# Scores from 64 rows per head in two PSUM banks, and token groups of 384 instead of 256

## The chip, the cores and the metric

The kernel runs on one core of one Trainium2 chip. The metric is the device time of one execution in microseconds. The core has TensorE (PE in the profile, with its weight loads as PEld), VectorE (DVE), ScalarE (ACT), GpSimd (POOL) and SyncE (SP), which here only issues DMA transfers. Matmuls write to PSUM, which has eight banks of 512 fp32 values in each of 128 partitions.

## The reference

Four batches, eight heads, 768 tokens, head size 64. Each token attends to the keys closer than 16 positions and to 24 block summaries (the maximum over 32 keys, the mean over 32 values); then comes a two-layer unit over all 3072 tokens.

```python
k_sum = k.reshape(B, H, nb, block, D).max(axis=3)       # block 32, nb 24
v_sum = v.reshape(B, H, nb, block, D).mean(axis=3)
scores_l = scale * np.matmul(q, k.transpose(0, 1, 3, 2))
mask_l = np.abs(pos[:, None] - pos[None, :]) < window   # window 16
scores_s = scale * np.einsum('bhsd,bhnd->bhsn', q, k_sum) + np.log(block)
a = softmax(concat(where(mask_l, scores_l, -1e9), scores_s))
attn = np.matmul(a, concat(v, v_sum))
x = attn.transpose(0, 2, 1, 3).reshape(B * S, H * D)    # 3072 x 512
out = np.maximum(x @ w1, x @ w2) @ w_out                # d_ff 1024
```

## The kernel before

**Tiles.** The work goes by batch, by pair of heads (four pairs), and within a pair by groups of 256 tokens (three of them). `prep` casts k and q to bf16 (`kqb`, line 340), turns them by TensorE (line 359) so that the 64 features of one head lie in partitions 0 to 63 and those of the other in 64 to 127, and places k in `kx` (line 373) and q in `qx` (line 388). `kx` holds for each tile of 64 keys 96 columns: 64 keys, 24 block maxima, 8 zeros; a window of 128 columns thus covers 64 keys, the summaries, and 32 keys of the next tile.

`qx` has two planes per head pair: in plane 0 the rows of the second head are zero, in plane 1 those of the first. The zeros are set once (lines 216 and 217). So one matmul of 128 rows gives the scores of both heads: the weights are the 128 columns of `kx`, and 2 x 64 queries stream through it (line 414). The last tile's queries wrap around the end of the sequence, so it takes two matmuls.

**A group.** `scores` fills one PSUM bank with 4 tiles x 2 heads x 64 queries, ACT takes the exponential of it into `pb` (line 426). Keys out of the window are hidden in one of two ways: in batch 0 by two matmuls of an identity with a pattern `hide` that is added to the scores in PSUM (line 403), in the other batches by a DVE multiplication of `pb` with a 0/1 `mask` (lines 435 and 441). `values` multiplies by `vx` (values, block means and a column of ones; line 460), DVE takes the reciprocal of the sums (line 472) and scales (line 474), TensorE turns x (line 484) and DVE copies it to `xt` (line 489).

**Maxout.** Since max(h1, h2) = h1 + relu(h2 - h1), the kernel makes `wd` = w2 - w1 once, and `w1o` = w1 @ w_out once (lines 506 to 544). For a group of 256 tokens, `maxout` computes x @ wd in four banks of two d_ff slices of 128 each (line 560), relu by ACT into `g` (line 565), and then for each 128 tokens x @ w1o (line 574) plus g @ w_out (line 581), one copy by ACT (line 340) and one store (line 592).

**Order.** Nothing is ordered by hand. `Plan` takes every operation with an engine, an estimated duration, its buffers and a priority, plays the execution through with those durations, and then issues the operations in the order in which they started there; each engine then runs its own list strictly in order. Attention of batch b has priority 1000 b, its maxout 1000 b + 1500 (lower goes first), so maxout of one batch fills TensorE's gaps in the attention of later ones. Buffers come from a `Ring` of slots; a buffer is taken when its first writer is planned and is free after its last user. The PSUM ring has eight single banks with caps by kind: two for turning k and q, two for scores, two for values, three for maxout.

Of the kernel before, what the change touches and what calls it, by code (L numbers as in the profile page):

```python
# [19 lines left out]
class Ring:  # L20
# [3 lines left out]
    def __init__(self, slots, cap=None, turn=None):  # L24
        self.slots, self.cap, self.turn = slots, cap or {}, turn
        self.owner = [None] * len(slots)

    def find(self, buf, now):
        live = [o is not None and o.end() > now for o in self.owner]
        if buf.kind in self.cap and self.cap[buf.kind] <= sum(  # L30
                o.kind == buf.kind for o, l in zip(self.owner, live) if l):
            return None
        if self.turn is not None and buf is not self.turn[0]:
            return None
        return min((s for s, l in enumerate(live) if not l), default=None, key=lambda s: (
            -1.0 if self.owner[s] is None else self.owner[s].end()))


class Buf:


    def __init__(self, ring, kind=None):
        self.ring, self.kind, self.slot = ring, kind, None
        self.writers, self.users = [], []
# [4 lines left out]
    def take(self, slot):  # L49
        self.slot, self.ring.owner[slot] = slot, self  # L50
        if self.ring.turn is not None:
            self.ring.turn.pop(0)
# [76 lines left out]
def kernel(  # L129
# [22 lines left out]
    NP, NT, NG, GT = H // 2, S // 64, 3, 256  # L152
# [12 lines left out]
    banks = Ring(list(range(8)), {"kq": 2, "sc": 2, "av": 2, "mm": 3})  # L165
# [9 lines left out]
    qxr = Ring(tiles("qx", 4, [128, 2, S], BF16))  # L175
    pbr = Ring(tiles("pb", 12, [128, 4, 192], BF16))
# [4 lines left out]
    xsr = Ring(tiles("xs", 4, [128, 2, 2, 2, D], BF16))  # L181
    xtr = Ring(tiles("xt", 6, [128, KC, GT], BF16))
    gr = Ring(tiles("g", 3, [128, FC, GT], BF16))
# [12 lines left out]
    hide = const.tile([128, 4, 64], BF16, name="hide")  # L196
    mask = const.tile([128, 4, 64], BF16, name="mask")
# [11 lines left out]
    def fixed_parts():  # L209
# [5 lines left out]
        def zero_qx(t):  # L215
            nc.vector.memset(t[0:64, 1], 0.0)
            nc.vector.memset(t[64:128, 0], 0.0)

# [6 lines left out]
        for i, t in enumerate(qxr.slots):  # L225
            once(qxr, i, 0.9, lambda t=t: zero_qx(t), i - 1)
        for i, t in enumerate(pbr.slots):
            once(pbr, i, 0.2, lambda t=t: nc.vector.memset(t[:, :, 64:128], 0.0), i / 3 - 1)
# [5 lines left out]
        def make_hide():  # L234

            nc.gpsimd.memset(hide[:], 0.0)
            for lo, hi, base in ((0, 64, -16), (96, 128, 96 - 48)):
                keep(hide[lo:hi], base + window - 1, 1, [[0, 4], [-1, 64]])  # L240
                keep(hide[lo:hi], window - 1 - base, -1, [[0, 4], [1, 64]])
            keep(hide[64:96], nb - 1, -1, [[0, 4], [0, 64]])
            nc.gpsimd.memset(hide[0:64, 3, 48:64], NEG)
            nc.gpsimd.memset(hide[96:128, 3, 0:48], NEG)
# [99 lines left out]
    def prep(b, hp, prio, k_on, q_on):  # L344
# [41 lines left out]
        for a in range(2):  # L386
            r = slice(64 * a, 64 * a + 64)
            op("ACT", 0.8, lambda a=a, r=r: nc.scalar.copy(  # L388
                out=qx[b, hp].ap[r, a, :], in_=order(qps)[r]),
               read=[qps], write=[qx[b, hp]], prio=prio, label=f"place q{tag}")  # L390

    def scores(b, hp, grp, prio, mask_on):


        ps, pb, tag = Buf(banks, "sc"), Buf(pbr), f"{b}{hp}{grp}"

        def view():
            return bank(ps).rearrange("p (i a w q) -> p i a w q", i=2, a=2, w=2)

        def mm():  # L400
            if mask_on == "PE":
                for i in range(2):
                    nc.tensor.matmul(
                        out=view()[:, i], lhsT=identity[:],
                        rhs=(hide[:, 2 * i:2 * i + 2] if grp == NG - 1 else hide[:, 0:2]).rearrange(
                            "p (o w) q -> p o w q", o=1).to_broadcast([128, 2, 2, 64]),
                        start=(i == 0), stop=False)
            for i in range(4):
                t = 4 * grp + i
                w = kx[b, hp].ap[:, 96 * t:96 * t + 128]  # L410
                at, o = 64 * t + 16, view()[:, i // 2, :, i % 2]
                for n0, n1 in ((0, 64),) if t < NT - 1 else ((0, 48), (48, 64)):
                    c = (at + n0) % S
                    nc.tensor.matmul(out=o[:, :, n0:n1], lhsT=w,  # L414
                                     rhs=qx[b, hp].ap[:, :, c:c + n1 - n0],
                                     start=(mask_on != "PE"),
                                     stop=(mask_on != "PE" or (i == 3 and n1 == 64)))

        op("PE", 0.25 + (0.23 if mask_on == "PE" else 0), mm, read=[kx[b, hp], qx[b, hp], hide_in],
           write=[ps], prio=prio, label=f"scores {tag}")  # L420

        def pv():
            a = pb.ap[:, :, 0:128]
            return bass.AP(a.tensor, a.offset, [a.ap[0], a.ap[1], [128, 2], [1, 64]])

        op("ACT", 0.7, lambda: nc.scalar.activation(  # L426
            out=pv(), in_=bank(ps).rearrange("p (i w q) -> p i w q", w=2, q=64),
            func=ACT.Exp, bias=bias[:], scale=scale),
           read=[ps], write=[pb], prio=prio, label=f"exp {tag}")

        def hidden_out():
            eng = nc.vector if mask_on == "DVE" else nc.gpsimd
            if grp < NG - 1:
                m = mask[:, 0:1].rearrange("p w (o q) -> p w o q", o=1).to_broadcast([128, 4, 2, 64])
                eng.tensor_tensor(out=pv(), in0=pv(), in1=m, op=ALU.mult)  # L435
            else:
                o = pv().rearrange("p (i a) w q -> p i a w q", a=2)
                for i in range(2):
                    m = mask[:, 2 * i:2 * i + 2].rearrange("p (o w) q -> p o w q", o=1).to_broadcast(
                        [128, 2, 2, 64])  # L440
                    eng.tensor_tensor(out=o[:, i], in0=o[:, i], in1=m, op=ALU.mult)

        if mask_on != "PE":
            op(mask_on, 0.43 if grp < NG - 1 else 0.56, hidden_out, read=[mask_in], change=[pb], prio=prio,
               label=f"mask {tag}")
        return pb
# [3 lines left out]
    def values(b, hp, grp, pb, prio):  # L450
        ps, tag = Buf(banks, "av"), f"{b}{hp}{grp}"

        def av():
            return bank(ps)[:, 0:4 * (D + 1)].rearrange("p (u a d) -> p u a d", u=2, a=2)

        def mm():
            for u in range(2):
                for a in range(2):
                    for par in range(2):
                        nc.tensor.matmul(out=av()[:, u, a, :],  # L460
                                         lhsT=pb.ap[:, 2 * u + a, 64 * par:64 * par + 128],
                                         rhs=vx[b].ap[:, 4 * grp + 2 * u + par, 2 * hp + a, 0:D + 1],
                                         start=(par == 0), stop=(par == 1))

        op("PE", 0.24, mm, read=[pb, vx[b]], write=[ps], prio=prio, label=f"values {tag}")
# [3 lines left out]
        if hp == 0:  # L469
# [4 lines left out]
        op("DVE", 0.42, lambda: nc.vector.tensor_tensor(  # L474
            out=x.ap[:, hp % 2], in0=av()[:, :, :, 0:D],
            in1=inv.ap[:].to_broadcast([128, 2, 2, D]), op=ALU.mult),
# [5 lines left out]
        def turn():  # L482
            for n in range(4):
                nc.tensor.transpose(out=bank(xp, 512, BF16)[:, 128 * n:128 * n + 128],  # L484
                                    in_=x.ap[:, n // 2, n % 2].rearrange("p a d -> p (a d)"),
                                    identity=identity[:])

        op("PE", 0.23, turn, read=[x], write=[xp], prio=prio, label=f"turn x{tag}")
        op("DVE", 0.42, lambda: nc.vector.tensor_copy(  # L489
            out=x_t.ap[:, hp - 1:hp + 1, :].rearrange("p h n -> p (h n)"),  # L490
            in_=bank(xp, 512, BF16)), read=[xp], write=[x_t], prio=prio, label=f"xt {tag}")

    invr = Ring(tiles("inv", 3, [128, 2, 2, 1], F32))
# [58 lines left out]
    def maxout(b, grp, prio):  # L552
        x, g = xt[b, grp], Buf(gr)
        for n in range(4):
            ps = Buf(banks, "mm")

            def hid(n=n, ps=ps):
                for s in range(2):
                    for c in range(KC):
                        nc.tensor.matmul(out=bank(ps)[:, 256 * s:256 * s + 256],  # L560
                                         lhsT=wd[n].ap[:, c, 128 * s:128 * s + 128],
                                         rhs=x.ap[:, c, :], start=(c == 0), stop=(c == KC - 1))

            op("PE", 0.88, hid, read=[x, wd[n]], write=[ps], prio=prio, label=f"hidden {b}{grp}{n}")
            op("ACT", 0.6, lambda n=n, ps=ps: nc.scalar.activation(  # L565
                out=g.ap[:, 2 * n:2 * n + 2, :].rearrange("p f n -> p (f n)"), in_=bank(ps),
                func=ACT.Relu), read=[ps], write=[g], prio=-1, label=f"relu {b}{grp}{n}")
        for u in range(2):
# [43 lines left out]
    def first_attention():  # L612

        pbs = {}
        for hp in range(NP):
            prep(0, hp, hp, *FIRST[hp])
            for grp in range(NG):
                pbs[hp, grp] = scores(0, hp, grp, (10, 110, 210)[grp] + hp, "PE")
        for grp in range(NG):
            for hp in range(NP):  # L620
                values(0, hp, grp, pbs[hp, grp], (20, 120, 220)[grp] + hp)
# [54 lines left out]
```

## Time and profile before

| | |
|---|---|
| runs | 193.31 us median of 3 (192.92 to 194.15) |
| profiled execution, span from the first to the last instruction | 192.5 us |
| what lies around the span, taken as median less span | 0.8 us |
| PE busy | 166.4 us, 1643 matmuls |
| ACT, DVE busy | 114.1 us, 109.9 us |
| data read and written | 25.17 MB, 6.29 MB |
| granted TensorE clock, mean | 0.991 |

The profile page lists one execution. It has no time of that execution beside its span, so the span is set against the median of the timed runs. The 40 slices show shares of the span in tenths; the chain of waits is followed back from the last instruction to whatever released each step. Matmuls are pipelined: the duration of one in the group list is much longer than the distance between two, which is seen in the chain as the length of a run divided by its matmuls.

### The profile page before, as it was taken

How to read it: one execution, taken by the hardware profiler on the slowest of the kernel's cores; microseconds unless marked ns; L12 is line 12 of the kernel's file. 1: busy time of each engine (PE TensorE's matmuls, PEld its weight loads, DVE VectorE, ACT ScalarE, POOL GpSimd, SP SyncE). 2: the span in 40 equal slices, each digit the busy share in tenths (PEclk: the TensorE clock that was granted, in tenths of full speed). 3: DMA queues.
4: the chain of work that ended last, by engine and by line, in shares of the span. 5: the costliest groups of instructions: out<-in, count | busy, mean ns of one | idle time of the engine just before them, and what ended most of it. 6: DMA issues, size and time to landing. Idle time of an engine off the chain costs nothing.

```text
span 192.5 us, 4148 instructions
## 1 busy us (share of the span) xinstructions
PE 166.4 (86%) x1643; PEld 117.9 (61%) x1664; DVE 109.9 (57%) x289; ACT 114.1 (59%) x173; POOL 25.7 (13%) x39
## 2 busy tenths in 40 slices
PE   0629619899999969999979999999999999999990
PEld 0426419865757738758657767487696676665740
DVE  6908956888979438759868953079777600000000
ACT  2533964384689949219967955179986443342621
POOL 7556221300330003300003300000000000000000
PEclk9999996999999999999999999999999999999999
DMA  5999999999999999999999996061020111120303
GB/s 187 226 305 356 234 240 347 371 381 281 210 359 251 292 268 217 339 309 217 229 288 223 340 218 193 3 164 24 3 109 5 54 58 59 50 109 0 112 0 109
DMA packets 47859, 37.27 MB, mean 194 GB/s; under 512 B 26208, under 2 KB 43744, under 8 KB 47840
## 3 DMA queue, kind: packets, MB, share of 16 engines
q1 hardware_dynamic: 47840, 37.01, 71.8%
q8 instruction: 13, 0.21, 0.5%
q14 instruction: 6, 0.05, 0.1%
HBM read 25.17 MB, written 6.29 MB: 163 GB/s over the span
## 4 chain that ended last, share of the span: by engine, by line
PE 53%; DMA 33%; SPq 5%; DVE 4%; POOL 2%; issue 1%; ACT 0%; ACTq 0%
PE banks L581 17%; PE banks L560 16%; DMA vf<-in_v_dram 13%; DMA vx<-vb 10%; PE banks L574 7%; PE banks L460 5%; DMA wf<-in_moe_w_out_dram 4%; SPq L503 4%; DMA vx<-vx 4%; PE banks L414 3%; DMA kqf<-in_k_dram 2%; PE banks L359 2%; POOL vb L340 2%; PE banks L484 2%; PE banks L313 1%; DVE pb L435 1%
## 5 line engine op out<-in xcount | busy, mean ns | idle before, releaser
L560 PE MATMUL banks<-xt,wd 128*128 128x256 bf16 x384 | 46.6, 273 | 0.5 <-DVE xt L489 0.5
L581 PE MATMUL banks<-wo,g 128*128 128x512 bf16 x184 | 44.9, 379 | 0.4
L560 PEld LDWEIGHTS <-wd 128*128 128x128 bf16 x384 | 36.4, 98 | 6.1 <-issue 0.7
L426 ACT ACTIVATE pb<-banks,bias 128x512 bf16<-128x512 f32 x48 | 31.5, 686 | 10.2 <-PE banks L414 9.9
L565 ACT ACTIVATE g<-banks 128x512 bf16<-128x512 f32 x48 | 28.3, 596 | 13.7 <-PE banks L560 13.2
L340 ACT COPY o<-banks 128x512 f32<-128x512 f32 x24 | 14.0, 585 | 28.7 <-PE banks L581 28.4
L388 ACT COPY qx<-banks 64x768 bf16<-64x768 bf16 x32 | 25.3, 791 | 6.1 <-PE banks L359 5.8
L581 PEld LDWEIGHTS <-g 128*128 128x128 bf16 x192 | 17.2, 97 | 16.5
L460 PE MATMUL banks<-vx,pb 128*128 128x65 bf16 x384 | 19.4, 196 | 3.6 <-DMA vx<-vx 1.8
L574 PE MATMUL banks<-w1o,xt 128*128 128x512 bf16 x85 | 21.9, 379 | 0.6
L460 PEld LDWEIGHTS <-pb 128*128 128x128 bf16 x384 | 16.9, 100 | 7.1 <-DMA vx<-vx 2.1
L359 PE MATMUL banks<-identity,kqb 128*128 128x128 bf16 x192 | 16.6, 234 | 5.3 <-DVE kqb L340 4.7
L340 ACT CAST kqb<-kqf 128x768 bf16<-128x768 f32 x16 | 13.1, 830 | 13.6 <-DMA kqf<-in_q_dram 8.7
L414 PE MATMUL banks<-qx,kx 128*128 128x128 bf16 (+2 forms) x208 | 18.6, 226 | 2.3 <-ACT qx L388 1.3
L340 POOL CAST vb<-vf 128x1536 bf16<-128x1536 f32 x8 | 12.2, 1520 | 55.0 <-DMA vf<-in_v_dram 35.2
L474 DVE TENSOR_TENSOR xs<-banks,inv 128x256 bf16<-128x256 f32 x48 | 19.1, 415 | 0.3
L414 PEld LDWEIGHTS <-kx 128*128 128x128 bf16 x208 | 15.1, 103 | 6.6 <-DVE kx L382 2.4
L359 PEld LDWEIGHTS <-kqb 128*128 128x128 bf16 x192 | 13.6, 106 | 8.5 <-DVE kqb L340 4.7
L373 DVE COPY kx<-banks 128x768 bf16<-128x768 bf16 x16 | 15.2, 955 | 2.9 <-PE banks L359 1.7
L375 DVE TENSOR_REDUCE ks<-kx 128x24 bf16<-128x768 bf16 x16 | 15.1, 944 | 0.1
L489 DVE COPY xt<-banks 128x512 bf16<-128x512 bf16 x24 | 9.8, 418 | 7.2 <-PE banks L484 6.8
L574 PEld LDWEIGHTS <-xt 128*128 128x128 bf16 x96 | 8.9, 98 | 7.9
(47 smaller groups left out, 129.8 us busy)
## 6 DMA issues: line engine op xcount, KB each, us to landing
kqf<-in_k_dram SPq DMA_DIRECT2D x16, 384.0 KB, 6.6
kqf<-in_q_dram SPq DMA_DIRECT2D x16, 384.0 KB, 5.7
vf<-in_v_dram SPq DMA_DIRECT2D x8, 768.0 KB, 10.7
out_dram<-o SPq DMA_DIRECT2D x20, 256.0 KB, 2.2
wf<-in_moe_w_dram SPq DMA_DIRECT2D x8, 512.0 KB, 11.1
vx<-vb SPq DMA_DIRECT2D x6, 396.0 KB, 8.0
wf<-in_moe_w_out_dram SPq DMA_DIRECT2D x4, 512.0 KB, 8.6
vx<-vx SPq DMA_DIRECT2D x4, 363.0 KB, 6.2
```

The source lines that it names most:

```text
L340: {"DVE": nc.vector.tensor_copy, "ACT": nc.scalar.copy, "POOL": nc.gpsimd.tensor_copy}[engine](out=o, in_=i)
L359: nc.tensor.transpose(out=bank(ps, S, BF16)[:, 128 * j:128 * j + 128], in_=src.ap[:, j].rearrange("p h d -> p (h d)"), identity=identity[:])
L373: op("DVE", 0.96, lambda: nc.vector.tensor_copy(out=kt()[:, :, 0:64], in_=order(kps)), read=[kps], write=[kx[b, hp], kmain], prio=prio, la ...
L388: op("ACT", 0.8, lambda a=a, r=r: nc.scalar.copy(out=qx[b, hp].ap[r, a, :], in_=order(qps)[r]), read=[qps], write=[qx[b, hp]], prio=prio, ...
L414: nc.tensor.matmul(out=o[:, :, n0:n1], lhsT=w, rhs=qx[b, hp].ap[:, :, c:c + n1 - n0], start=(mask_on != "PE"), stop=(mask_on != "PE" or (i ...
L426: op("ACT", 0.7, lambda: nc.scalar.activation(out=pv(), in_=bank(ps).rearrange("p (i w q) -> p i w q", w=2, q=64), func=ACT.Exp, bias=bias ...
L460: nc.tensor.matmul(out=av()[:, u, a, :], lhsT=pb.ap[:, 2 * u + a, 64 * par:64 * par + 128], rhs=vx[b].ap[:, 4 * grp + 2 * u + par, 2 * hp ...
L474: op("DVE", 0.42, lambda: nc.vector.tensor_tensor(out=x.ap[:, hp % 2], in0=av()[:, :, :, 0:D], in1=inv.ap[:].to_broadcast([128, 2, 2, D]), ...
L560: nc.tensor.matmul(out=bank(ps)[:, 256 * s:256 * s + 256], lhsT=wd[n].ap[:, c, 128 * s:128 * s + 128], rhs=x.ap[:, c, :], start=(c == 0), ...
L565: op("ACT", 0.6, lambda n=n, ps=ps: nc.scalar.activation(out=g.ap[:, 2 * n:2 * n + 2, :].rearrange("p f n -> p (f n)"), in_=bank(ps), func ...
L574: nc.tensor.matmul(out=bank(ps), lhsT=x.ap[:, c, sl], rhs=w1o[c].ap[:], start=(c == 0), stop=False)
L581: nc.tensor.matmul(out=bank(ps), lhsT=g.ap[:, f, sl], rhs=wo[f // 2].ap[:, f % 2, :], start=False, stop=(f == FC - 1))
```

## The change

Three things are changed together.

- `qx` has one plane and no zeros. Scores are computed for each head by its own matmul of 64 rows (partitions 0 to 63 for one head, 64 to 127 for the other) and 64 query columns, into a PSUM bank of its own. A scores buffer is therefore two adjacent banks, and `Ring` learns to hand out such pairs.
- Attention and maxout go in two groups of 384 tokens instead of three of 256. So exp takes 768 elements per row at once, values fill 6 x 65 columns, `hide` and `mask` are 6 tiles wide; maxout takes one d_ff slice of 384 tokens per bank (eight matmul groups and eight relus instead of four), and three output tiles of 128 tokens per group instead of two.
- The numbers of buffers follow: `pb` 8 instead of 12, `xt` 4 instead of 6, `g` 2 instead of 3, each half as large again. The plan's estimated durations are set to the new sizes.

```diff
-    NP, NT, NG, GT = H // 2, S // 64, 3, 256
+    NP, NT, NG, GU = H // 2, S // 64, 2, 3
+    GT = 128 * GU
...
+        if buf.wide:
+            return min((s for s in range(0, len(live), 2) if not live[s] and not live[s + 1]),
+                       default=None, key=lambda s: max(self.freed(s), self.freed(s + 1)))
         return min((s for s, l in enumerate(live) if not l), default=None, key=lambda s: (
-            -1.0 if self.owner[s] is None else self.owner[s].end()))
+            self.pairs and not live[s ^ 1], self.freed(s)))
...
-    qxr = Ring(tiles("qx", 4, [128, 2, S], BF16))
-    pbr = Ring(tiles("pb", 12, [128, 4, 192], BF16))
+    qxr = Ring(tiles("qx", 4, [128, S], BF16))
+    pbr = Ring(tiles("pb", 8, [128, 2 * GU, 192], BF16))
...
-        def zero_qx(t):
-            nc.vector.memset(t[0:64, 1], 0.0)
-            nc.vector.memset(t[64:128, 0], 0.0)
...
-        for a in range(2):
-            r = slice(64 * a, 64 * a + 64)
-            op("ACT", 0.8, lambda a=a, r=r: nc.scalar.copy(
-                out=qx[b, hp].ap[r, a, :], in_=order(qps)[r]),
-               read=[qps], write=[qx[b, hp]], prio=prio, label=f"place q{tag}")
+        op("ACT", 0.8, lambda: nc.scalar.copy(
+            out=qx[b, hp].ap[:].rearrange("p (c j) -> p c j", j=J), in_=order(qps)),
+           read=[qps], write=[qx[b, hp]], prio=prio, label=f"place q{tag}")
...
-        ps, pb, tag = Buf(banks, "sc"), Buf(pbr), f"{b}{hp}{grp}"
+        ps, pb, tag = Buf(banks, "sc", wide=True), Buf(pbr), f"{b}{hp}{grp}"
...
-            for i in range(4):
-                t = 4 * grp + i
-                w = kx[b, hp].ap[:, 96 * t:96 * t + 128]
...
-                    nc.tensor.matmul(out=o[:, :, n0:n1], lhsT=w,
-                                     rhs=qx[b, hp].ap[:, :, c:c + n1 - n0],
...
+            for i in range(2 * GU):
+                t = 2 * GU * grp + i
                 for n0, n1 in ((0, 64),) if t < NT - 1 else ((0, 48), (48, 64)):
...
+                    for a in range(2):
+                        r = slice(64 * a, 64 * a + 64)
+                        nc.tensor.matmul(out=view()[:, a, 64 * i + n0:64 * i + n1],
+                                         lhsT=kx[b, hp].ap[r, 96 * t:96 * t + 128],
+                                         rhs=qx[b, hp].ap[r, c:c + n1 - n0],
...
-        for n in range(4):
+        for n in range(FC):
             ps = Buf(banks, "mm")
 
             def hid(n=n, ps=ps):
-                for s in range(2):
-                    for c in range(KC):
-                        nc.tensor.matmul(out=bank(ps)[:, 256 * s:256 * s + 256],
-                                         lhsT=wd[n].ap[:, c, 128 * s:128 * s + 128],
-                                         rhs=x.ap[:, c, :], start=(c == 0), stop=(c == KC - 1))
+                for c in range(KC):
+                    nc.tensor.matmul(out=bank(ps, GT), lhsT=wd[n // 2].ap[:, c, 128 * (n % 2):128 * (n % 2) + 128],
+                                     rhs=x.ap[:, c, :], start=(c == 0), stop=(c == KC - 1))
```

129 lines of the change are left out of this document (64 added, 65 removed).

## The prediction

> **What bounds the kernel now.** I read the page first: its span, the busy shares and the 40 slices; then the time windows, then TensorE's waits, then the chain of waits in order of time.
>
> ```profile
> span 192.5 us, 4148 instructions
> PE 166.4 (86%) x1643; PEld 117.9 (61%) x1664; DVE 109.9 (57%) x289; ACT 114.1 (59%) x173; POOL 25.7 (13%) x39
> ...
> PEclk9999996999999999999999999999999999999999
> DMA  5999999999999999999999996061020111120303
> ```
>
> TensorE is the busiest engine, and the transfer engines are full for the first 24 slices (115 us). A busy share over the whole span doesn't say which of the two sets the end, so I cut the span where values of batch 0 are running (34.3), where values of batch 2 begin (97.36) and where the last matmuls end (188.1).
>
> ```profile
> 0.00:34.30 34.30, 18.53 (x183) 14.40 (x184) 22.93 (x59) 17.81 (x24) 15.16 (x29) 0.95 1.03 272
> 34.30:97.36 63.06, 58.33 (x617) 41.40 (x627) 48.13 (x118) 42.77 (x64) 7.41 (x8) 1.00 1.08 288
> 97.36:188.10 90.74, 89.56 (x844) 62.13 (x855) 38.86 (x113) 52.92 (x86) 3.17 (x2) 1.00 0.38 102
> 188.10:192.50 4.40, 0.00 (x0) 0.00 (x0) 0.00 (x0) 0.58 (x1) 0.00 (x0) 1.00 0.36 119
> ```
>
> Columns are start:end, length, busy time of PE, PEld, DVE, ACT and POOL, granted clock, DMA share, GB/s. Up to 34.3 TensorE is busy for half the time and the transfers set the pace. From 34.3 on it is busy for 58.33 + 89.56 = 147.9 of 153.8 us at full clock. What it waited for there, all told:
>
> ```profile
> PE banks L460 <- DMA vx<-vx: 1.8, 1, 1.8
> PE banks L460 <- DMA kqf<-in_k_dram: 1.3, 1, 1.3
> PE banks L560 <- DVE xt L489: 0.5, 1, 0.5
> PE banks L460 <- DVE pb L435: 0.5, 1, 0.5
> PE banks L544 <- ACT wo L340: 0.4, 1, 0.4
> PE banks L313 <- POOL vb L340: 0.3, 1, 0.3
> ```
>
> 3.1 us for transfers (one at 69, one at 96 us) and only 1.7 us for DVE, ACT and POOL. So after 34.3 the amount of TensorE work sets the end nearly one for one; making DVE or ACT faster can return at most that 1.7 us. Behind the last matmul there are 4.4 us of one copy and one store, of the same size after the change.
>
> **TensorE's prices.** These are lengths of runs in the chain, thus start to start, not the pipelined durations of the page.
>
> ```profile
> 75.28 0.24 PE banks L460 x8
> 110.82 0.45 PE banks L414 x8
> 112.13 0.23 PE banks L414 x5
> 161.99 3.49 PE banks L560 x32
> 167.21 3.45 PE banks L581 x16
> 188.09 0.58 ACT o L340
> ```
>
> Per matmul with its own weight load: 65 columns (L460) 0.24/8 = 0.030 us; 128 columns (L414) 0.45/8 = 0.056; 256 columns (L560) 3.49/32 = 0.109; 512 columns (L581) 3.45/16 = 0.216. So 0.00042 us per column, (0.216 - 0.109)/256, and 0.002 besides. How far down does that go? The smallest matmul of the trace has 32 columns:
>
> ```profile
> 149.15 0.18 PE L414 MATMUL banks<-qx,kx 128*128 128x32 bf16 x1
> 149.18 0.59 PE L581 MATMUL banks<-wo,g 128*128 128x512 bf16 x2
> ```
>
> Its successor starts 0.03 us later, as behind 65 columns, though 32 columns alone would be 0.015. One load and one matmul don't go below about 0.03 us, however few the columns.
>
> **The change, part by part.**
>
> *Scores.* A head pair now takes 13 matmuls (12 tiles, the last one split), 0.45 + 0.23 = 0.68 us. Afterwards each becomes two, of 64 rows and half the columns: 26. One after another at the 0.03 of the nearest rows this is 0.78 us, +0.10. If the two of a pair, at different row positions, run beside each other, it is 13 x 0.03 = 0.39 us, -0.29. The trace has no matmul with fewer than 128 rows, so it doesn't decide; and the switch between 64 and 128 rows may have a price of its own (a rival below). I take one after another: every row of this kernel that has a load per matmul sits at 0.03 or above. How many head pairs count:
>
> ```profile
> 34.30:97.36 63.06, 5.17 (x65) 4.36 (x65) 1.00 1.08 288
> 97.36:188.10 90.74, 7.31 (x91) 5.82 (x91) 1.00 0.38 102
> ```
>
> These are the same windows for the scores line alone: 65/13 = 5 head pairs up to 97.36 and 7 behind it. So +0.10 x 12 = +1.2 us. The first 5 come ahead of values that wait for transfers anyway (1.8 and 1.3 us), so their 0.5 us is covered; without that cover it counts in full. Batch 0's four head pairs lie before 34.3 under the transfers. Its hidden-key matmuls are 16 of 384 columns in place of 24 of 256, the same 6144 columns.
>
> *Maxout.* 384 matmuls of 256 columns become 256 of 384: 0.002 + 384 x 0.00042 = 0.163 us each, 41.7 against 384 x 0.109 = 41.9: about -0.2 us. The second matmuls (L574, L581), values, transposes, weights' work and stores keep number and size.
>
> *ACT, DVE, POOL.*
>
> ```profile
> L426 ACT ACTIVATE pb<-banks,bias 128x512 bf16<-128x512 f32 x48 | 31.5, 686 | 10.2 <-PE banks L414 9.9
> L565 ACT ACTIVATE g<-banks 128x512 bf16<-128x512 f32 x48 | 28.3, 596 | 13.7 <-PE banks L560 13.2
> L388 ACT COPY qx<-banks 64x768 bf16<-64x768 bf16 x32 | 25.3, 791 | 6.1 <-PE banks L359 5.8
> L474 DVE TENSOR_TENSOR xs<-banks,inv 128x256 bf16<-128x256 f32 x48 | 19.1, 415 | 0.3
> L216 DVE MEMSET qx<- 64x384 uint32 x4 | 1.5, 378 | 0.1
> L217 DVE MEMSET qx<- 64x384 uint32 x4 | 1.5, 378 | 0.5
> ```
>
> Placing q: 16 copies instead of 32, of the same 768 elements a row, so 16 x 0.79 = 12.7 us less. Exp: 32 of 768 elements, each between 0.69 and 1.5 x 0.69 = 1.03 us, so 22 to 33 us against 48 x 0.686 = 32.9. Relu: 64 of 384, each between 0.45 and 0.60 us, 29 to 38 against 28.6. ACT gives up some 13 us, at least 3. DVE loses the zeroes of q (3.0 us, all before 9 us) and 16 of 48 normalisations that become half again as long. None of it is on the path after 34.3: in the last dense window DVE is busy for 38.9 and ACT for 52.9 of 90.7 us. I cost it at nothing; the cover is the maxout matmuls that the plan puts between. Were it gone, a longer exp or normalisation would hold a group back by up to 0.34 or 0.2 us, 14 groups behind 97.36: up to 5 us.
>
> ```profile
> 1.71 2.30 POOL L231 TENSOR_SCALAR_AFFINE_SELECT hide<-hide 64x256 bf16<-64x256 bf16 x5
> 9.25 1.47 POOL L340 CAST vb<-vf 128x1536 bf16<-128x1536 f32 x1 [1.84 <-DMA vf<-in_v_dram]
> ```
>
> The hidden-key pattern is half as wide again: up to 1.2 us more on POOL, ahead of the v cast, where POOL idles 1.84 us for v. Nothing. No DMA is added or removed.
>
> *PSUM.* A scores group takes two adjacent banks, so two groups in flight take four of eight. A group that waits for a free pair holds TensorE's whole list, the values and maxout matmuls written behind it, and ACT's exp after those. I cost it at nothing, between no effect and the rival below.
>
> *Sum.* +1.2 - 0.5 - 0.2 = about +0.5 us on a span of 192.5, so 193.0. The median of the runs, 193.31, lies 0.8 us above the span; with the same 0.8 the time is **193.8 us**: no change that can be measured (I take 1%, 1.9 us, as the limit).
>
> **Rivals.**
>
> *The pairs overlap.* 0.39 us per head pair: -0.29 x 7 = -2.0 behind 97.36, up to -1.5 before it (or that is lost in longer waits for transfers), -0.2 for maxout: 193.3 - 2.2 to 193.3 - 3.7, so 189.6 to 191.1, say **190.4**. For it: the two use different rows, operands and banks. Against: the floor of 0.03 us under the 32-column matmul looks like the load's or the issue's, and there are twice as many of both. [...]
>
> *Each switch of row height empties TensorE.*
>
> ```profile
> L460 PE MATMUL banks<-vx,pb 128*128 128x65 bf16 x384 | 19.4, 196 | 3.6 <-DMA vx<-vx 1.8
> L414 PEld LDWEIGHTS <-kx 128*128 128x128 bf16 x208 | 15.1, 103 | 6.6 <-DVE kx L382 2.4
> ```
>
> A 65-column matmul lasts 0.196 us though the next starts after 0.030, so 0.17 us of each is hidden by its successor; a switch could expose that, and the load's 0.10. After 34.3 there are 24 scores groups: 48 switches if each stands alone, 24 if two of a head pair stand together. At 0.17 that is 4 to 8 us, at 0.27 up to 13; on top of +0.5, less what the transfer waits swallow, some +4.5: **197.8**, slower. It decides from about 0.06 us a switch (36 x 0.06 = 2.2) if pairs don't overlap. Against: transposes and matmuls alternate without a visible price, but both have 128 rows. [...] With both, overlap and emptying, the sum is -3.7 + 4 to 8, so 193.6 to 197.6, say **195**.
>
> *Order.* Larger groups and bank pairs make the written-out order stall in more places. The longest wait now is 1.8 us; two more like it give **197**. Against: the waits for DVE, ACT and POOL are 1.7 us in all.
>
> **How the numbers follow.** One after another without a price of switching, 0.35; overlap alone, 0.30; emptying alone, 0.15; both, 0.12; order, 0.08. Faster by over 1% (below 191.4): nine tenths of the overlap case and a little of the forecast, 0.30. Slower (above 195.2): emptying, half of both, most of the order case and a little of the forecast, 0.30. Within: 0.40. The forecast's own range is 191.8 to 195.4; the range that holds overlap to its lower bound and the centre of emptying is 189.4 to 198.0, with some 0.15 outside.
>
> **What would show it.** Runs of scores in the chain: 26 matmuls in 0.78 us (forecast) or 0.4 (overlap). A gap, or a late first matmul, at each border between scores and other work: emptying. In the wait list, waits of scores for exp (a bank pair not free) or longer waits of values: order. TensorE's dense stretch must still run from about 34 to within 4.4 us of the end; if it starts 2 us earlier or later, the start, not the prices, made the difference and the prediction is wrong for a reason that it doesn't have.

## The result, and the profile after

The changed kernel takes 200.25 us (median of 4 runs, 198.2 to 202.56) against 193.2 us before: 1.031 times as long, interval 1.023 to 1.039. The range forecast ended at 198.0. The profiled execution of the changed kernel is its longest run, 202.56 us with a span of 200.8, and the only one of it that has a profile, so its waits may be longer than a typical run's. In this run 1.8 us lie around the span; the 0.8 us of the table ahead of the prediction is a median less the span of one run. The forecast isn't touched by that: it adds 0.5 us to the median of 193.31. Repeats of the same program differ more here than I had assumed: the runs of before lie between 191.2 and 199.1 us over all comparisons. In what follows medians are of all runs, while ratios and their intervals leave out runs more than 1.5% above the fastest of their kernel.

The page of the changed kernel: span, TensorE's busy time, granted clock and DMA share in 40 slices.

```profile
span 200.8 us, 4201 instructions
PE 167.7 (84%) x1719; PEld 101.5 (51%) x1736; DVE 101.0 (50%) x225; ACT 99.3 (49%) x157; POOL 26.1 (13%) x39
...
PEclk9999985699999999999999759999999999999997
DMA  5999999999999999999999980035002102102122
```

ACT gave up time as worked out (114.1 to 99.3 us); DVE (109.9 to 101.0) and the weight loads (117.9 to 101.5) gave up some too; the transfers are as before. The clock dips in slices 6 to 8, where the kernel before has one dip (slice 7), and, newly, in slices 23 and 24. The same cuts as for the kernel before, at the start of batch 0's and batch 2's values and at the last matmul:

```profile
0.00:34.70 34.70, 16.23 (x199) 9.94 (x200) 20.52 (x40) 14.29 (x17) 15.93 (x29) 0.91 1.02 279
34.70:96.95 62.25, 57.37 (x653) 36.71 (x659) 43.24 (x97) 34.61 (x54) 7.23 (x8) 0.97 1.11 279
96.95:196.40 99.45, 94.12 (x869) 54.85 (x877) 37.19 (x90) 49.84 (x87) 2.94 (x2) 0.97 0.37 100
196.40:200.80 4.40, 0.00 (x0) 0.00 (x0) 0.00 (x0) 0.57 (x1) 0.00 (x0) 0.77 0.20 60
```

Batch 2's values start at the same time as before (96.95 and 97.36), set by the transfers. The stretch behind them is 99.45 us instead of 90.74: there the 8.3 us of the two spans appear. TensorE's waits, changed kernel (in total, times, longest):

```profile
PE banks L460 <- DMA vx<-vx: 4.7, 2, 2.7
PE banks L516 <- POOL w1b L343: 4.7, 2, 2.8
PE banks L316 <- POOL vb L343: 4.4, 1, 4.4
PE banks L414 <- ACT pb L427: 4.2, 1, 4.2
PE banks L362 <- ACT kqb L343: 2.4, 2, 1.3
PE banks L484 <- DVE xs L474: 1.2, 2, 1.0
```

**The wait of 4.2 us at 110 us.** Scores wait for exp. ACT's and TensorE's lists there, in order of time:

```profile
108.66 0.83 ACT L343 CAST kqb<-kqf 128x768 bf16<-128x768 f32 x1 [4.41 <-DMA kqf<-in_q_dram]
112.36 0.83 ACT L343 CAST kqb<-kqf 128x768 bf16<-128x768 f32 x1 [2.87 <-DMA kqf<-in_q_dram]
113.10 1.68 ACT L427 ACTIVATE pb<-banks,bias 128x768 bf16<-128x768 f32 x2
```

```profile
114.04 0.51 PE L414 MATMUL banks<-qx,kx 64*128 64x64 bf16 x12 [4.19 <-ACT pb L427]
```

The exps of batch 2 stand in ACT's list behind two casts of q of batch 3, and those wait for their transfers. TensorE's next scores need the bank pair that the first exp is to free. Every engine was right to wait; the list was in the wrong order. That the plan expects the loads too early is the likely reason; no run alters that alone.

**The late start.** Batch 0's values wait for the block means, which DVE copies out of PSUM and one transfer spreads. DVE's copy, the issue of the transfer and the values on TensorE, first before, then after:

```profile
18.62 0.69 DVE L319 CAST vx<-banks 32x512 bf16<-32x512 f32 x1
```

```profile
19.34 0.62 SPq L327 DMA_DIRECT2D vx<-vx  x1
```

```profile
29.80 1.09 PE L460 MATMUL banks<-vx,pb 128*128 128x65 bf16 x16
```

```profile
22.65 0.69 DVE L322 CAST vx<-banks 32x512 bf16<-32x512 f32 x1
```

```profile
23.38 1.37 SPq L330 DMA_DIRECT2D vx<-vx  x1
```

```profile
34.76 2.08 PE L460 MATMUL banks<-vx,pb 128*128 128x65 bf16 x35 [1.97 <-DMA vx<-vx]
```

In DVE's list two placings of k now stand ahead of the means instead of one. The copy is 4.0 us later, the spread is issued behind five of the weights' loads instead of two, and the values run at 34.76 instead of 29.80 (a single matmul of them starts at 32.53).

**The clock.** The windows around both places, changed kernel and then before (the column ahead of the DMA share is the granted clock):

```profile
30.00:40.00 10.00, 5.58 (x85) 5.19 (x85) 6.33 (x13) 1.78 (x2) 2.19 (x3) 0.58 1.08 329
110.00:120.00 10.00, 5.64 (x67) 3.80 (x68) 3.56 (x10) 5.37 (x8) 0.00 (x0) 0.67 0.97 228
```

```profile
30.00:40.00 10.00, 9.49 (x146) 8.63 (x144) 8.27 (x23) 4.91 (x7) 2.19 (x3) 0.87 1.07 365
110.00:120.00 10.00, 9.89 (x101) 7.25 (x102) 4.91 (x16) 5.68 (x10) 0.00 (x0) 1.00 0.91 223
```

A clock of 0.67 over ten microseconds can cost up to 3.3 us, on top of the wait itself. At 110 us half clock (0.50 granted) runs from 113.5 to 120.3 us, beginning 0.6 us before the wait of 4.2 us ends. In the kernel before it runs from 29.3 to 32.7 us, behind a wait of 4.0 us that ends at 28.64; behind waits of at most 1.8 us after 34 us the clock stayed at 1.00 up to the last matmul. At the late start of the changed kernel half clock runs from 28.1 to 38.4 us with single waits of only 2.8, 1.9 and 2.0 us, and in a later run (the changed kernel with the means first, repeated) the clock between 30 and 40 us is 0.83, with single waits of 0.7 and 1.7 us up to 34 us, and behind the second 12 values take 0.68 us instead of 0.37. A wait isn't always followed by it either: in the changed kernel the clock stayed at 1.00 behind a wait of 2.7 us that ends at 70.03, and behind two of 4.8 and 4.4 us that end before 15 us. What decides it isn't shown by these runs.

**Added up.** The clock's share below is an estimate: TensorE's busy time in each microsecond, times the part of the clock that was missing in it. Between 25 and 45 us TensorE idles for 7.4 us instead of 4.5 and loses 3.0 us to half clock instead of 1.7, so the late start costs some 4.2 us. Behind batch 2's first values it idles for 5.3 us instead of 1.2 and loses 3.0 us instead of nothing, so the place at 110 us costs some 7.1 us. The rest of its busy time is some 3 us shorter than before (161.7 against 164.7). Together this is the 8.3 us of the spans: in this execution the work of TensorE got shorter, and waits and clock took back more.

**Scores themselves.** A stretch of the changed kernel's TensorE timeline (start, length with the last one's pipeline, what):

```profile
92.13 0.50 PE L362 MATMUL banks<-identity,kqb 128*128 128x128 bf16 x6
92.47 0.81 PE L559 MATMUL banks<-xt,wd 128*128 128x384 bf16 x4
93.12 0.50 PE L362 MATMUL banks<-identity,kqb 128*128 128x128 bf16 x6
93.55 0.53 PE L414 MATMUL banks<-qx,kx 64*128 64x64 bf16 x26
94.01 0.51 PE L362 MATMUL banks<-identity,kqb 128*128 128x128 bf16 x6
...
143.80 0.35 PE L414 MATMUL banks<-qx,kx 64*128 64x64 bf16 x12
144.08 1.04 PE L572 MATMUL banks<-w1o,xt 128*128 128x512 bf16 x3
145.05 0.35 PE L414 MATMUL banks<-qx,kx 64*128 64x64 bf16 x14
145.33 0.51 PE L362 MATMUL banks<-identity,kqb 128*128 128x128 bf16 x6
```

26 matmuls take 94.01 - 93.55 = 0.46 us and 14 take 145.33 - 145.05 = 0.28, both with transposes behind them, so 12 more cost 0.18: 0.015 each, 0.03 a pair. The single starts in the trace say the same: the two of a pair start 3 to 4 ns apart, and a pair starts 0.029 us behind the last one. Pairs do overlap; without borders a head pair would take 13 x 0.029 = 0.38 us. But the first transpose behind a run starts 0.098 us after the last score, and the 512-column matmul at 144.08 starts 0.122 us after it, where within a run the next pair starts 0.026 us after the last score. And the six transposes ahead of a run take 0.43 us (93.12 to 93.55) where the same six take 0.34 ahead of maxout (92.13 to 92.47): 0.09 at its start. So a switch of row height costs about 0.1 us each way, some 0.18 us a run. After 34.7 there are 16 runs for 12 head pairs: 0.38 + 16/12 x 0.18 = 0.62 us per head pair, against 0.68. Both effects that the prediction named as rivals of its forecast are in the trace: the two matmuls of a pair, at different row positions, run beside each other (0.029 us a pair), and a switch costs time (some 0.18 us a run). Here they nearly cancel.

### The profile page after: what moved, and what is told of

Read it like the earlier page. It is cut to its first block, busy times and chain, and to the rows that moved or that the text cites. A ratio compares the mean times of both kernels' runs of the same rounds, so it can differ in the third digit from the quotient of the medians.

```text
span 200.8 us, 4201 instructions
## 1 busy us (share of the span) xinstructions
PE 167.7 (84%) x1719; PEld 101.5 (51%) x1736; DVE 101.0 (50%) x225; ACT 99.3 (49%) x157; POOL 26.1 (13%) x39
## 4 chain that ended last, share of the span: by engine, by line
PE 64%; DMA 19%; DVE 11%; issue 2%; ACT 1%; POOL 1%; SPq 1%; ACTq 0%; DVEq 0%
PE banks L559 19%; PE banks L579 17%; DMA vx<-vx 10%; PE banks L572 8%; PE banks L460 6%; DMA vf<-in_v_dram 5%; DMA kqf<-in_q_dram 4%; PE banks L316 3%; DVE kx L376 3%; PE banks L362 3%; PE banks L544 3%; PE banks L484 3%; DVE ks L378 2%; PE banks L414 2%; DVE kx L382 1%
## 5 line engine op out<-in xcount | busy, mean ns | idle before, releaser
L559 PE MATMUL banks<-xt,wd 128*128 128x384 bf16 x256 | 48.2, 329 | 0.0
L579 PE MATMUL banks<-wo,g 128*128 128x512 bf16 x185 | 45.7, 383 | 0.9 <-issue 0.7
L563 ACT ACTIVATE g<-banks 128x384 bf16<-128x384 f32 x64 | 31.2, 495 | 17.2 <-PE banks L559 16.0
L559 PEld LDWEIGHTS <-wd 128*128 128x128 bf16 x256 | 23.9, 99 | 14.7 <-issue 0.9
L427 ACT ACTIVATE pb<-banks,bias 128x768 bf16<-128x768 f32 x32 | 27.8, 904 | 7.0 <-PE banks L414 7.0
L474 DVE TENSOR_TENSOR xs<-banks,inv 128x384 bf16<-128x384 f32 x32 | 17.4, 550 | 0.4
L389 ACT COPY qx<-banks 128x768 bf16<-128x768 bf16 x16 | 12.6, 798 | 5.6 <-PE banks L362 5.6
L414 PE MATMUL banks<-qx,kx 64*128 64x64 bf16 (+2 forms) x416 | 10.8, 197 | 4.9 <-ACT pb L427 4.2
L414 PEld LDWEIGHTS <-kx 64*128 64x128 bf16 x416 | 8.3, 100 | 12.4 <-issue 8.6
L472 DVE RECIPROCAL inv<-banks 128x6 f32<-128x6 f32 x32 | 6.0, 191 | 12.0 <-PE banks L460 11.5
## 6 DMA issues: line engine op xcount, KB each, us to landing
vx<-vb SPq DMA_DIRECT2D x6, 396.0 KB, 10.2
```

What stands on the lines that cost most here:

```text
L414: nc.tensor.matmul(out=view()[:, a, 64 * i + n0:64 * i + n1], lhsT=kx[b, hp].ap[r, 96 * t:96 * t + 128], rhs=qx[b, hp].ap[r, c:c + n1 - n0 ...
L427: op("ACT", 0.9, lambda: nc.scalar.activation(out=pv(), in_=view().rearrange("p a (u w q) -> p a u w q", w=2, q=64), func=ACT.Exp, bias=bi ...
L474: op("DVE", 0.56, lambda: nc.vector.tensor_tensor(out=x.ap[:, hp % 2], in0=av()[:, :, :, 0:D], in1=inv.ap[:].to_broadcast([128, GU, 2, D]) ...
L559: nc.tensor.matmul(out=bank(ps, GT), lhsT=wd[n // 2].ap[:, c, 128 * (n % 2):128 * (n % 2) + 128], rhs=x.ap[:, c, :], start=(c == 0), stop= ...
L563: op("ACT", 0.5, lambda n=n, ps=ps: nc.scalar.activation(out=g.ap[:, n, :], in_=bank(ps, GT), func=ACT.Relu), read=[ps], write=[g], prio=- ...
L579: nc.tensor.matmul(out=bank(ps), lhsT=g.ap[:, f, sl], rhs=wo[f // 2].ap[:, f % 2, :], start=False, stop=(f == FC - 1))
```

## The experiments

Theory A: the loss is in the written-out order, at the two places above, with the clock's share. Theory B: switching row height costs it. Theory C: the coarse groups and bank pairs cost it. All comparisons are with the kernel before on the same chip.

| kernel | median us (runs) | to before, interval |
|---|---|---|
| rows only, groups of 256 | 199.4 (4) | 1.028 (1.019 to 1.036) |
| groups of 384 only, q padded | 196.14 (10) | 1.006 (1.001 to 1.011) |
| changed, means first | 191.48 (4) | 0.987 (0.978 to 0.996) |
| the same, again | 192.25 (12) | 0.994 (0.990 to 0.998) |
| changed, q cast on POOL | 196.92 (4) | 1.015 (1.008 to 1.023) |
| order kept, means moved | 197.49 (4) | 1.020 (1.012 to 1.029) |
| order kept, q casts moved | 196.7 (10) | 1.016 (1.011 to 1.022) |
| order kept, both moved | 198.46 (4; 195.0 to 200.5) | none: too scattered |
| both moved, rows in turn | 199.18 (4; 195.0 to 201.7) | none: too scattered |
| changed, zeros kept | 197.2 (4) | 1.020 (1.008 to 1.032) |
| changed, longer estimate for placing q | 196.63 (6) | 1.016 (1.011 to 1.021) |
| before, means first | 193.84 (10) | 0.997 (0.992 to 1.002) |
| rows only, means first | 194.05 (10) | 1.004 (0.999 to 1.009) |
| groups only, means first | 194.18 (10) | 1.006 (1.001 to 1.011) |
| changed, means first, longer estimate for loads | 191.17 (6) | 0.987 (0.983 to 0.991) |
| the same, again | 191.03 (6) | 0.988 (0.982 to 0.993) |
| changed, means first, q cast on POOL | 192.42 (6) | 0.990 (0.983 to 0.996) |
| before, means first, longer estimate for loads | 193.91 (12) | 1.001 (0.997 to 1.005) |

### Each part alone

Rows only: the changed kernel with `NG, GU = 3, 2`, the buffer counts, estimates and `maxout` of before.

> The changed kernel with its scores of 64 rows in two banks, but groups of 256 tokens and the maxout of before. Theory A (the loss is in the written-out order, at two places: block means of batch 0 that come late, and ACT's list held up by casts of q that wait for transfers): a head pair's scores take some 0.5 us instead of 0.68, worth up to 2 us; where the order has neither stall 190 to 193 us, where it has them 196 to 200. Theory B (switching between 64 and 128 rows costs): three scores groups per head pair instead of two, so even more borders, slower than 198. Theory C (groups of 384 make the stalls): 190 to 193 us, no wait over 2 us.

Groups only: q in two planes with zeros again; a bank holds every second tile of both heads.

```diff
...
-                    for a in range(2):
-                        r = slice(64 * a, 64 * a + 64)
-                        nc.tensor.matmul(out=view()[:, a, 64 * i + n0:64 * i + n1],
-                                         lhsT=kx[b, hp].ap[r, 96 * t:96 * t + 128],
-                                         rhs=qx[b, hp].ap[r, c:c + n1 - n0],
+                    nc.tensor.matmul(out=o[:, :, n0:n1], lhsT=kx[b, hp].ap[:, 96 * t:96 * t + 128],
+                                     rhs=qx[b, hp].ap[:, :, c:c + n1 - n0],
...
```

> The changed kernel with groups of 384 tokens and bank pairs, but q padded with zeros again and scores of 128 rows and 2 x 64 columns, 13 matmuls per head pair. Theory A: PE work as before, the order decides: 193 to 200 us, and the profile shows the same kind of waits if it is slow. Theory B: about 193 us. Theory C: 198 us or more, with waits of 2 us and more after 34 us.

Rows only is as slow as the whole change, 199.4 us, and its means are late in the same way (copied at 22.94 us):

```profile
36.32 0.87 PE L460 MATMUL banks<-vx,pb 128*128 128x65 bf16 x13 [1.99 <-DMA vx<-vx]
```

It has no stall at 110 us: behind 30 us its scores wait at most 0.3 us for exp. So the late start alone can go with a loss of this size. Groups only has a ratio of 1.006, though its ten runs spread from 193.4 to 199.3 us and their median is 1.3% above before; its means are copied early:

```profile
18.80 0.69 DVE L328 CAST vx<-banks 32x512 bf16<-32x512 f32 x1
```

This speaks against theory C as the main cause, and means first below settles it, since that keeps the coarse groups and the bank pairs. The loss goes with the part that holds the rows and q's single placing. That is where theory B would put it as well; the next runs separate them.

### The two places

Means first:

```diff
-           read=[ps], write=[vx[b], mean], prio=prio + 2, label=f"means {b}")
+           read=[ps], write=[vx[b], mean], prio=prio + (2 if b else 0), label=f"means {b}")
```

> The changed kernel with one number altered: the priority of DVE's copy of batch 0's block means goes ahead of the placing of k. Theory A: the means are spread some 4 us earlier, values of batch 0 start at about 30 instead of 34.8 us, the half clock between 30 and 40 us shortens; 2 to 4 us less, 196 to 198 us, if the stall at 110 us stays. Theories B and C: no change, 200 us.

It fell by 8.8 us, to 191.48 (from 1.031 to 0.987 of before), more than twice what was expected, with the same operations and all scores still in 64 rows: neither theory B nor theory C can be the main cause. The plan came out otherwise from there on; in the repeat's profile the values start at 25.32 and ACT's stall is gone too.

```profile
25.32 0.69 PE L460 MATMUL banks<-vx,pb 128*128 128x65 bf16 x12
```

```profile
110.00:120.00 10.00, 9.95 (x82) 5.74 (x80) 3.09 (x8) 3.62 (x8) 0.00 (x0) 1.00 0.54 110
```

q cast on POOL:

```diff
-            prep(b, hp, p, "DVE", "ACT")
+            prep(b, hp, p, "DVE", "POOL")
```

> The changed kernel with the casts of q of batches 1 to 3 on POOL instead of ACT. Theory A: ACT's exp no longer stands behind a cast that waits for a transfer, the wait of 4.2 us at 110 us and the half clock behind it (about 3 us) go: 5 to 7 us less, 193 to 195 us. Theories B and C: no change, 200 us.

196.92 us, 3.3 less where 5 to 7 were expected; scores no longer wait for exp, the late start stays.

Both edits change the whole plan. To alter single places, I kept the changed kernel's written order and moved two operations each time, just before the operations are issued:

```diff
+        self.move(order, ('DVE', 'means 0', ('DVE', 'spread v01')))
+        self.move(order, ('SP', 'spread means 0', ('SP', 'load w1')))
...
+        self.move(order, ('ACT', 'cast q31', ('ACT', 'exp 231')))
+        self.move(order, ('ACT', 'cast q32', ('ACT', 'cast q31')))
```

> The changed kernel's written order, unaltered but for two operations: DVE's copy of batch 0's block means goes right behind DVE's two spreads of v, and the transfer that spreads the means goes behind two of the weights' loads instead of five. Theory A (two stalls, each with its own cause): values of batch 0 start 3 to 5 us earlier (34.8 before), less half clock before 40 us; 2 to 4 us less than the changed kernel's 200, and the wait of 4 us at 110 us stays. Theory D (the early delay alone also sets the later stall): the stall at 110 us goes as well, 192 us or less.

> The changed kernel's written order, unaltered but for two operations: ACT's casts of q of the second and third head pairs of batch 3 go behind the four exps of batch 2 that followed them. Theory A: the 4.2 us wait of scores for exp at 110 us and the half clock behind it go: 5 to 7 us less, 193 to 195 us; the late start at 34.8 us stays. Theory D: the PE waits elsewhere for the same transfers, 198 us or more.

> Both moves together in the changed kernel's order. Theory A: the gains add, 189 to 192 us, below the 193.2 of the kernel before, since scores take 0.2 us less per head pair. Theory B (switching between row heights costs): no better than 193 us.

Means moved: 197.49. The transfer is issued at 18.07 us, yet the values run only at 33.58, since in TensorE's kept list they stand behind transposes that wait for weights. The stall at 110 us shrank too, from 4.19 to 0.54 us, because the transfers behind the casts came 2 to 3 us earlier: the second place depends in part on the first. That is half of theory D; the time it gave, 192 us or less, didn't come.

```profile
33.58 1.26 PE L469 MATMUL banks<-vx,pb 128*128 128x65 bf16 x36
...
111.18 0.35 PE L423 MATMUL banks<-qx,kx 64*128 64x64 bf16 x12 [0.54 <-ACT pb L436]
```

q casts moved: 196.7, and the scores run through at 109 us without a wait:

```profile
107.53 1.90 PE L588 MATMUL banks<-wo,g 128*128 128x512 bf16 x8
109.36 0.35 PE L423 MATMUL banks<-qx,kx 64*128 64x64 bf16 x12
```

Each move returned 3 us, about as theory A said of the first and less than it said of the second. Both together missed: 198.46 us, 195.0 to 200.5, where 189 to 192 was expected. By this run alone theory B would stand; it is means first, with the same switches of row height, that speaks against it. In the profiled run of both (198.28 us) no scores wait for exp, but the values still start only at 33.84 us, the clock between 30 and 40 us is 0.66, and values wait 3.7 us for transfers:

```profile
30.00:40.00 10.00, 7.39 (x127) 5.93 (x126) 8.26 (x16) 3.77 (x4) 2.19 (x3) 0.66 1.07 367
```

So mending places in a fixed list doesn't add up. Which share of its scatter is the clock's isn't settled.

### How the rows overlap

With both moved, and the tiles of one head listed ahead of those of the other:

```diff
-            for i in range(2 * GU):
...
-                    for a in range(2):
+            for a in range(2):
+                r = slice(64 * a, 64 * a + 64)
+                for i in range(2 * GU):
```

> As the kernel with both moves, the same written order, but in each scores group all tiles of one head come first and then all of the other, so that neighbours in TensorE's list use the same rows. If pairs overlap only between neighbours at different rows, a head pair's 26 matmuls take 0.78 us and more instead of 0.46: some 0.3 x 12 = 3 to 4 us longer than with both moves. If the list order doesn't matter, the same time.

The times are too scattered to say anything; the timeline says it. 26 matmuls from 97.02 to 97.58 are 0.56 us, 0.10 more than in pairs and far less than 0.78:

```profile
97.02 0.63 PE L425 MATMUL banks<-qx,kx 64*128 64x64 bf16 x26
97.58 0.51 PE L373 MATMUL banks<-identity,kqb 128*128 128x128 bf16 x6
```

So most of the gain (0.22 of 0.32 us) came without the two of a pair side by side in the list.

### What moved the means

> The changed kernel with the zeroing of q's padding kept as plain work on DVE: the same eight memsets with the same priorities, on a tile that nobody reads. If taking these zeroes away is what moved batch 0's block means behind the placing of k in DVE's list, the means come earlier again and the values start at 26 to 31 us: 192 to 197 us. If something else of the change moved them, 198 to 201 us with values at 34 us or later.

```diff
+    qzr = Ring(4 * tiles("qz", 1, [128, 2, S], BF16))
...
+        for i, t in enumerate(qzr.slots):
+            once(qzr, i, 0.9, lambda t=t: zero_qz(t), i - 1)
```

Not the zeroes: with them the means are copied at 22.95, as late as without. The time, 197.2 us, lies between the two ranges expected; in its profile scores wait 2.5 us for exp instead of 4.2.

```profile
22.95 0.69 DVE L329 CAST vx<-banks 32x512 bf16<-32x512 f32 x1
```

Next suspect: placing q is planned with 0.8 us of ACT instead of two times 0.8, so ACT casts the next q sooner, the transposes of the third head pair's k come sooner, and its placing is ready on DVE, with a better priority, when the means are.

```diff
-        op("ACT", 0.8, lambda: nc.scalar.copy(
+        op("ACT", 0.8 if b else 1.6, lambda: nc.scalar.copy(
```

> The changed kernel with one estimate of the plan altered: placing q of batch 0 is planned with 1.6 us, as the two copies of before took, instead of 0.8; the work itself is unaltered. If the shorter placing of q is what let k of the third head pair reach DVE ahead of the means, the means are copied at about 17 us instead of 22.7, the values of batch 0 start at 25 to 31 us, and the time falls to 191 to 197 us. If not, it stays at 198 to 201 us.

```profile
18.79 0.69 DVE L322 CAST vx<-banks 32x512 bf16<-32x512 f32 x1
```

That is it: with this one number and the same work the copy is at 18.79 us, values run at 30.49 us, and the time falls to 196.6. It did not fall further: TensorE's new list has its own waits for transfers (8.8 us in three).

### Is the change worth anything under a better order?

> The kernel before, with the same altered priority of batch 0's block means. If the early order alone made the kernel with means first (191.5 us) faster than before, this one comes to 190 to 192 us as well. If that gain needed the change's shorter scores and fewer, larger operations, this one stays at 192 to 194 us.

> 64-row scores with groups of 256 and the maxout of before, and means first. Scores of a head pair save 0.3 us by overlap and lose some 0.18 us at each run of scores, of which there are more in three groups than in two: within 1 us of the before kernel with means first. Values of batch 0 start at 25 to 31 us instead of 36, so 4 us or more less than rows only (199.4): 192 to 195 us.

> Padded q and 128-row scores in groups of 384, and means first. Without switches of row height and without overlap, TensorE's work is within 1 us of that of the changed kernel: 190 to 193 us if the order has no wait over 2.5 us after 34 us; each further wait adds itself and up to 3 us of half clock. If the 64 rows themselves are worth something, some 1 us longer than the changed kernel with means first (191.5).

> The changed kernel with means first, repeated. If it really beats the kernel before: 190 to 192.5 us, 1% or more below it on the same chip. If the first result was luck: within 0.5% of the before kernel, as the three other combinations with means first were.

With means first the four combinations come to 193.8 (neither part), 194.1 (rows), 194.2 (groups, above the 190 to 193 expected) and 192.3 us (both, twelve runs, on another chip). Against before on the same chip these are 0.997, 1.004, 1.006 and 0.994. The first 191.48 was partly luck. Neither part gains alone, and that both together gain isn't clear from these runs: the intervals of 0.997 and 0.994 overlap.

> Means first, and loads of k and q of batches 1 to 3 planned with 2.1 us instead of 1.05. If the short estimate is what puts casts of q ahead of exps in ACT's list too early, no scores wait for exp for over 1 us and the waits of values for transfers (2.3 and 1.4 us with means first) shrink: 189 to 191.5 us. If the estimate doesn't matter: as means first, 191 to 192 us.

```diff
-            op("SP", 1.05, lambda f=f, src=src: nc.sync.dma_start(
+            op("SP", 1.05 if b == 0 else 2.1, lambda f=f, src=src: nc.sync.dma_start(
```

> Means first, and the casts of q of batches 1 to 3 on POOL. If ACT's list still cost something with means first: 1 us or more below it. If the stall went already with the other order: the same within 1 us, 190 to 193 us.

> The kernel before with means first and the loads of k and q of later batches planned with 2.1 us. If the change itself is worth nothing under an order of equal quality: 190.5 to 192 us, within 0.5% of the changed kernel with the same two numbers. If the change is worth its shorter work on TensorE (under 1 us) and its fewer operations: 192 to 194 us.

> The changed kernel with means first and the longer estimate for loads, repeated: 190 to 192 us, some 1% below the kernel before.

The longer estimate for loads gives 191.17 and 191.03 us, the fastest version, 1.2 to 1.3% below before. By itself 191.17 fits both ranges expected, but after 30 us values no longer wait for transfers. The kernel before with the same two numbers stays at 193.91. So with these two numbers the change is worth some 2.9 us on the same chip. The fastest version's profile has waits of at most 1.6 us after 30 us, of at most 1.1 us after 37 us, and no dip of the clock before the last matmul:

```profile
span 189.0 us, 4178 instructions
PE 163.1 (86%) x1718; PEld 97.9 (52%) x1736; DVE 101.8 (54%) x225; ACT 98.4 (52%) x157; POOL 26.0 (14%) x39
...
PEclk9999999999999999999999999999999999999997
```

The stretch behind 97 us up to the last matmul, the fastest version and then the kernel before with both numbers, each at full clock:

```profile
97.00:184.50 87.50, 86.71 (x819) 50.40 (x828) 35.30 (x84) 46.13 (x80) 3.24 (x2) 1.00 0.46 125
```

```profile
97.00:187.50 90.50, 89.86 (x843) 62.07 (x853) 38.58 (x116) 52.67 (x85) 2.95 (x2) 1.00 0.44 121
```

It is 3.0 us shorter, and TensorE's busy time in it 3.2. How much of that is shorter work, and how much is work that this order does ahead of 97 us, isn't settled: scores and maxout as measured above account for about 1 us.

q on POOL beside means first: 192.42 us, no difference to means first alone, as expected if that stall had gone already.

## Why the prediction was wrong, point by point

**What bounds the kernel.** "After 34.3 the amount of TensorE work sets the end nearly one for one" held only as long as the dense stretch begins at 34 and has no waits. Neither is a property of the work; both are the order's. The prediction named a start that moves by 2 us or more as the way in which it could fail for a reason that it doesn't have, and that happened: the values start 5 us later.

**ACT, DVE, POOL: "I cost it at nothing".** This is the step that failed. The sizes were right (ACT 14.8 us less, forecast some 13). But shorter ACT work isn't neutral in a kernel whose lists are written from estimated durations: a halved estimate for placing q put two placings of k ahead of the block means (shown by changing that one number: 3.6 us less), and the casts of q stood ahead of exps whose banks TensorE needed (shown by moving the two casts alone: 3.6 us less). In the profiled execution the two places cost some 4.2 and 7.1 us. Which part of the change put the casts there wasn't isolated; rows only doesn't have that stall.

**The rival "order".** It had the right mechanism and 0.08, and the signs that the prediction gave for it came: scores that wait for exp, and longer waits of values. It was priced at 197 from two more waits of 1.8 us; measured were one of 4.2 us, a start 5 us later, and half clock at both places. The clock was in none of the terms, though the first fence of the prediction shows a dip in slice 7.

**Scores.** One after another at 0.03 was wrong: a pair takes 0.029 us, so a load and a matmul of 64 rows take half of the floor that the prediction read from the 32-column row. A free switch was wrong too: about 0.1 us each way. Both rivals were half of the truth; the sum per head pair is -0.06 us instead of +0.10, some 1.9 us less over 12 head pairs, so this term can't have made the kernel slower. The point of 0.06 us per switch, from which emptying would decide, was worked out for pairs that don't overlap.

**Maxout and PSUM.** 384 columns take 0.163 us as forecast (four in 92.47 to 93.12 is 0.65). Bank pairs: the one long wait of scores for exp is a pair that isn't free, because exp came late, not because banks were few; with the casts moved it is gone.

**Chances.** Slower had 0.30 against 0.30 for faster; the direction was left open and the upper bound was 2 us short, since it held the one switching rival and not the order.

## What to carry to other kernels

Where lists are written from a plan, a change of any estimate rewrites the order on every engine: before a small gain is forecast from busy times, ask which operation on the path has a rival on its own engine that becomes ready sooner, and what in-order list holds a wait for a transfer ahead of work that TensorE needs. A wait on TensorE is to be priced with the half clock that can come with it: the waits of 4.0 us (before, up to 28.64) and 4.2 us (changed, up to 114.04) came with 3.4 and 6.8 us of it, and three of 1.9 to 2.8 us between 24 and 35 us (changed) with 10.2 us, while one of 2.7 us at 70 us had none. Splitting the padded matmul into two of half the rows gained here by overlap about what it lost at the borders: with its borders a head pair costs some 0.55 us in one run of 26 and 0.75 in two runs (estimates from 13 pairs of 0.029 us and 0.18 us a run), against 0.68 padded.

## What the runs showed of the hardware that I had not expected

Two 64-row matmuls at different row positions, each with its own weight load, step by 0.029 us a pair at 64 columns, and switching between 64 and 128 rows cost about 0.1 us in each direction. Listing one head's tiles ahead of the other's cost only 0.10 us per 26 matmuls (0.56 against 0.46), where one after another at 0.03 they would take 0.78. Half clock lasted 10.2 and 6.8 us in one execution of the changed kernel (0.58 granted between 30 and 40 us, 0.67 between 110 and 120), at the first place with single waits of only 1.9 to 2.8 us.
